# Loading each 128-token block with its own DMA, 4 KB reads on the DRAM side

## The chip, the cores and the metric

One core of a Trainium2 chip. The metric is the time of one execution in microseconds on the device; lower is better.

## The reference, cut to what matters

```python
def _attn_ref(x, f_logit, lower_bound):        # x, f_logit: (4, 6336, 256) float32
    f = lower_bound + (1.0 - lower_bound) * sigmoid(f_logit)
    i = 1.0 - f
    for t in range(S):                         # a recurrence along the sequence
        h = f[:, t] * h + i[:, t] * x[:, t]
        y[:, t] = h
def _moe_ref(x, w_h, w_t, b_t):                # on y, 25344 tokens x 256
    H = maximum(x @ w_h, 0);  T = sigmoid(x @ w_t + b_t)
    return T * H + (1 - T) * x
```

52 MB are read and 26 MB written.

## The kernel before

The work is cut into 25 units. Unit 0 has 768 tokens; units 1 to 24 have 1,024 tokens each, as eight blocks of 128. The loads of a full unit are two DMAs of 1 MB on the sync queue (SP); its output goes out in two stores of 512 KB on the same queue. Names: `lt` is f_logit in SBUF, `xt` is x, `u` the sigmoid (the gate), `bv` the product u*x, `y` the scan, `d` and `e` two multiplications after it, `o` the output. In the profile's lines PE is TensorE, PEld its weight loads, DVE VectorE, ACT ScalarE, POOL GpSimd; a q behind a name (SPq) is the list of instructions that issues for that engine.

```python
inp  = tc.tile_pool(name="inp",  bufs=4)      # lt, xt, u: four buffers each
outp = tc.tile_pool(name="outp", bufs=2)      # o: two buffers

def load(n):
    ...
    for src, t in ((f_logit, lt), (x, xt)):
        if len(segs) == 1:                    # a full unit
            b, s0, _, ln = segs[0]
            pin(nc.sync.dma_start(t, src[b, s0:s0 + ln, :].rearrange("(j p) d -> p j d", p=np_)))
        else: ...                             # unit 0: two loads of 384 KB per tensor

def gate(n):    ... ScalarE: u = sigmoid(-lt)           # reads all of lt
def product(n): ... GpSimd: bv = u * xt, in four pieces
def scan(n, h): ... VectorE: y = scan(f, bT)            # 1,024 steps, two halves h
def o_act(n, q):
    ... ScalarE: o[:, half q] = copy(PSUM)
    nc.sync.dma_start(out_bsd[b, a:a + ln // 2, :].rearrange("(j p) d -> p j d", p=np_), oq)

for n in range(-3, NU + 2):                   # one iteration, cut:
    load(n + 4)
    ... o_act(n - 2, 0) ... gate(n + 2) ... o_act(n - 2, 1) ...
    ... product(n + 2)                        # each engine runs its part in this order
```

All DMAs of this program (they are issued by SyncE and ScalarE) share eight completion semaphores in turn (numbers 100 to 107 in the trace), and a ninth DMA is not issued until the oldest of the eight has landed: in the traces before the change no DMA is issued with more than seven others out. At the start this is a wait of 3.0 us (below).

Of the kernel before, what the change touches and what calls it, by code (L numbers as in the profile page):

```python
# [19 lines left out]
def kernel(  # L20
# [16 lines left out]
    nc = tc.nc  # L37
    B, S, D = x.shape
# [3 lines left out]
    NB = 8  # L42
# [21 lines left out]
    def pin(ins):  # L64
        return tc.keep_in_program_order(ins)

    def load(n):
        np_, segs = units[n]
        lt = inp.tile([P, NB, D], FP32, tag="lt")
        xt = inp.tile([P, NB, D], FP32, tag="xt")  # L70
        for src, t in ((f_logit, lt), (x, xt)):
            if len(segs) == 1:
                b, s0, _, ln = segs[0]
                pin(nc.sync.dma_start(t, src[b, s0:s0 + ln, :].rearrange("(j p) d -> p j d", p=np_)))
            else:
                t4 = t.rearrange("p (b j) d -> p b j d", j=2)
                for j in range(2):
                    nc.sync.dma_start(
                        t4[:np_, :, j, :],
                        src[:, j * np_:(j + 1) * np_, :].rearrange("b p d -> p b d"))  # L80
        st[n]["lt"], st[n]["xt"] = lt, xt

    load(0)
    load(1)

    ident_b = singles.tile([P, P], BF16, name="ident_b")
# [7 lines left out]
    for h in range(NH):  # L94
        for vec, t in ((lower_bound, lb), (moe_b_t, bt)):
            nc.scalar.dma_start(t[:, h:h + 1], bass.AP(
                tensor=vec.tensor, offset=vec.offset + h * P, ap=[[1, P], [1, 1]]))
# [149 lines left out]
    for n in range(-3, NU + 2):  # L247
        if ok(n + 4) and n + 4 > 1:
            load(n + 4)
# [70 lines left out]
```

## Time and profile before

| | before |
|---|---|
| time, median of 2 (range) | 236.41 us (235.45 to 237.36) |
| one unit in steady state | 8.19 us (spacing of the e products) |
| VectorE busy there | 39.5 of 40 us |
| DMA rate there | 384 GB/s; the highest of the page's 40 slices is 388 |

The busy time of each engine in three stretches of steady state (busy us and number of instructions per engine, then the granted clock, the DMA share and GB/s):

```profile
core 0: us, PE busy (x) PEld busy (x) DVE busy (x) ACT busy (x) POOL busy (x), PEclk, DMA share, GB/s
60.00:100.00 40.00, 36.59 (x398) 25.79 (x397) 39.48 (x25) 38.41 (x35) 21.70 (x20) 1.00 1.09 384
100.00:140.00 40.00, 36.96 (x395) 25.81 (x393) 39.48 (x25) 38.39 (x35) 21.70 (x20) 1.00 1.09 384
```

VectorE (DVE) is full, ScalarE (ACT) nearly so, and the DMA engines are full too. The chain of waits, by engine and line:

```profile
DVE 77%; issue 6%; PE 5%; ACT 2%; DVEq 0%; ACTq 0%
DVE y L161 45%; DVE d L199 20%; DVE e L206 12%; PE zp L175 1%; PE gp L190 1%; ACT o L233 1%; ACT t L183 1%; PE op L224 1%; PE op L223 1%; PE bT L150 0%; PE uT L136 0%; DVE e L209 0%; DVEq L206 0%; ACTq L233 0%; DVEq L209 0%
```

VectorE's scan and its two multiplications carry the chain ("issue" is time in which the engine waited for nothing that the profile shows); no DMA is on it. The DMA issues (count, size, median us from issue to landing):

```profile
DMA packets 78805, 78.68 MB, mean 334 GB/s; under 512 B 2240, under 2 KB 78784, under 8 KB 78784
...
lt<-in_f_logit_dram SPq DMA_DIRECT2D x24, 1024.0 KB, 9.3
xt<-in_x_dram SPq DMA_DIRECT2D x24, 1024.0 KB, 10.6
out_dram<-o SPq DMA_DIRECT2D x48, 512.0 KB, 7.9
```

The sync queue in one unit of steady state (start, duration, what):

```profile
64.76 1.28 SPq L74 DMA_DIRECT2D lt<-in_f_logit_dram  x1
66.13 2.57 SPq L74 DMA_DIRECT2D xt<-in_x_dram  x1
68.79 4.23 SPq L237 DMA_DIRECT2D out_dram<-o  x2
```

An issue of 1 MB takes 2.57 us, which is 1 MB at 408 GB/s: the queue is not working that long, it is held back while the DMA engines still have work: 105 to 160 rows of 1 KB are queued for each of them (5th to 95th percentile at an issue from 60 to 180 us, counted in the packet records). It is ahead of them. And two waits of the sync queue:

```profile
SPq L237 <- ACT o L233: 58.6, 28, 4.5
...
SPq L78 <- DMA lb<-in_lower_bound_dram: 3.0, 1, 3.0
```

The second is the limit of eight: the third load of the queue waits 3.0 us for the tiny lower_bound load, which has nothing to do with it, at a time when eight DMAs are out. In the trace's semaphore numbers the two share one (100).

### The profile page before, as it was taken

To read this page: it belongs to the slowest core of one execution; us is meant where nothing else is said; L and a number is where in the kernel's file an instruction comes from. 1 tells how busy PE (TensorE), PEld (TensorE's weight loads), DVE (VectorE), ACT (ScalarE), POOL (GpSimd) and SP (SyncE) were. 2 spreads that over 40 slices of the span, in tenths; PEclk is the share of its full clock that TensorE was granted. 3 is DMA by queue.
4 is the path that set the end of the run, shared out by engine and by line. 5 is a ranking of instruction groups with operands and counts; after the bars stand their busy time and mean duration, and the time that the engine had idled before them with its cause. 6 is when DMAs were issued, how large, how long until landed. Compare 5 with 4: busy or idle time off the path is not lost.

```text
span 235.8 us, 4853 instructions
## 1 busy us (share of the span) xinstructions
PE 192.1 (81%) x2000; PEld 134.5 (57%) x2000; DVE 203.6 (86%) x144; ACT 198.3 (84%) x176; POOL 114.2 (48%) x108
## 2 busy tenths in 40 slices
PE   0135899898999989899998989898999989897751
PEld 0125566666566666667566666656666666665441
DVE  0425799999999999999999999999999999999540
ACT  0645789999999999999999999999999999975541
POOL 1088553574376357436634753673475357430000
PEclk9999999999999999999999999999999999999985
DMA  6999999999999999999999999999999995243255
GB/s 150 302 386 386 386 383 386 379 385 383 382 386 383 386 382 386 384 384 379 386 386 382 385 383 383 379 382 375 385 383 386 388 368 205 97 152 119 89 178 177
DMA packets 78805, 78.68 MB, mean 334 GB/s; under 512 B 2240, under 2 KB 78784, under 8 KB 78784
## 3 DMA queue, kind: packets, MB, share of 16 engines
q1 hardware_dynamic: 77664, 77.86, 94.4%
q10 hardware_dynamic: 1120, 0.53, 0.9%
q8 instruction: 15, 0.25, 0.4%
q14 instruction: 6, 0.05, 0.0%
HBM read 52.43 MB, written 25.95 MB: 332 GB/s over the span
## 4 chain that ended last, share of the span: by engine, by line
DVE 77%; issue 6%; PE 5%; ACT 2%; DVEq 0%; ACTq 0%
DVE y L161 45%; DVE d L199 20%; DVE e L206 12%; PE zp L175 1%; PE gp L190 1%; ACT o L233 1%; ACT t L183 1%; PE op L224 1%; PE op L223 1%; PE bT L150 0%; PE uT L136 0%; DVE e L209 0%; DVEq L206 0%; ACTq L233 0%; DVEq L209 0%
## 5 line engine op out<-in xcount | busy, mean ns | idle before, releaser
L126 POOL TENSOR_TENSOR bv<-u,xt 128x512 bf16<-128x512 f16 (+1 forms) x100 | 113.2, 1164 | 93.7 <-DVE e L206 72.9
L161 DVE TENSOR_TENSOR_SCAN y<-f,y,bT 128x1024 bf16<-128x1024 f16 x48 | 112.3, 2341 | 2.6 <-ACT t L183 1.4
L183 ACT ACTIVATE t<-zp,bt 128x1024 bf16<-128x1024 f32 (+1 forms) x50 | 55.3, 1106 | 13.6 <-PE zp L175 10.6
L199 DVE SCALAR_TENSOR_TENSOR d<-y,ncc,gp 128x1024 bf16<-128x1024 bf16 (+1 forms) x50 | 62.2, 1244 | 2.5 <-PE gp L190 2.5
L144 ACT ACTIVATE f<-uT,ncc 128x1024 f16<-128x1024 f16 (+1 forms) x50 | 55.9, 1117 | 5.5 <-PE uT L136 5.5
L233 ACT COPY o<-op 128x1024 f32<-128x1024 f32 (+1 forms) x50 | 50.2, 1005 | 5.7 <-PE op L224 5.7
L190 PE MATMUL gp<-y,w_sb 128*128 128x512 bf16 (+1 forms) x200 | 51.5, 380 | 4.0 <-DVE d L199 1.4
L223 PE MATMUL op<-diag,y 128*128 128x128 f16 (+1 forms) x400 | 50.9, 221 | 2.2 <-ACT o L233 2.2
L175 PE MATMUL zp<-y,w_sb 128*128 128x512 bf16 (+1 forms) x200 | 51.6, 381 | 0.3 <-ACT t L183 0.3
L224 PE MATMUL op<-ident_b,e 128*128 128x128 bf16 (+1 forms) x400 | 50.8, 221 | 0.5 <-DVE e L206 0.5
L119 ACT ACTIVATE u<-lt 128x2048 f16<-128x2048 f32 (+1 forms) x25 | 47.5, 1902 | 2.1 <-DMA lt<-in_f_logit_dram 2.1
L150 PE MATMUL bT<-ident_b,bv 128*128 128x128 bf16 (+1 forms) x400 | 31.7, 222 | 20.8 <-DVE y L161 16.5
L224 PEld LDWEIGHTS <-e 128*128 128x128 bf16 (+1 forms) x400 | 39.7, 100 | 8.8 <-DVE e L206 1.9
L223 PEld LDWEIGHTS <-y 128*128 128x128 bf16 (+1 forms) x400 | 39.8, 100 | 5.7
L150 PEld LDWEIGHTS <-bv 128*128 128x128 bf16 (+1 forms) x400 | 26.8, 99 | 27.5 <-issue 20.0
L136 PE MATMUL uT<-ident_h,u 128*128 128x128 f16 (+1 forms) x400 | 32.2, 227 | 11.0 <-ACT u L119 10.0
L190 PEld LDWEIGHTS <-w_sb 128*128 128x128 f16 x200 | 19.6, 98 | 24.4 <-issue 7.1
L136 PEld LDWEIGHTS <-u 128*128 128x128 f16 (+1 forms) x400 | 26.0, 103 | 11.4 <-ACT u L119 10.0
L206 DVE TENSOR_TENSOR e<-d,t 128x2048 bf16<-128x2048 bf16 x24 | 29.4, 1225 | 2.9 <-DVE d L199 0.5
L175 PEld LDWEIGHTS <-w_sb 128*128 128x128 f16 x200 | 18.7, 99 | 18.2 <-issue 1.1
L161 DVE TENSOR_TENSOR_SCAN y<-f,bT 128x192 bf16<-128x192 f16 x8 | 3.8, 534 | 7.3 <-PE bT L150 7.3
L119 ACT ACT_TABLE_LOAD x1 | 1.3, 1283 | 6.7 <-DMA lt<-in_f_logit_dram 6.7
(15 smaller groups left out, 5.7 us busy)
## 6 DMA issues: line engine op xcount, KB each, us to landing
lt<-in_f_logit_dram SPq DMA_DIRECT2D x24, 1024.0 KB, 9.3
xt<-in_x_dram SPq DMA_DIRECT2D x24, 1024.0 KB, 10.6
out_dram<-o SPq DMA_DIRECT2D x48, 512.0 KB, 7.9
lt<-in_f_logit_dram SPq DMA_DIRECT2D x2, 384.0 KB, 5.0
xt<-in_x_dram SPq DMA_DIRECT2D x2, 384.0 KB, 5.7
out_dram<-o SPq DMA_DIRECT2D x2, 384.0 KB, 6.6
w_raw<-in_moe_w_h_dram ACTq DMA_DIRECT2D x1, 256.0 KB, 4.8
w_raw<-in_moe_w_t_dram ACTq DMA_DIRECT2D x1, 256.0 KB, 5.4
```

The lines of the kernel that those rows point to most:

```text
L126: ins = pin(nc.gpsimd.tensor_mul(bv[:np_, q:q + 2], st[n]["u"][:np_, q:q + 2], st[n]["xt"][:np_, q:q + 2]))
L136: pin(nc.tensor.transpose(uT[:, j * np_:(j + 1) * np_], st[n]["u"][:np_, j, h * P:(h + 1) * P], ident_h[:np_, :np_]))
L144: pin(nc.scalar.activation(st[n]["f"][:, h, :N], st[n]["uT"][:, :N], AF.Identity, scale=ncc[:, h:h + 1], bias=1.0))
L150: pin(nc.tensor.transpose(bT[:, j * np_:(j + 1) * np_], st[n]["bv"][:np_, j, h * P:(h + 1) * P], ident_b[:np_, :np_]))
L161: pin(nc.vector.tensor_tensor_scan(y[:, h, c0:c0 + ln], st[n]["f"][:, h, c0:c0 + ln], st[n]["bT"][:, c0:c0 + ln], 0.0 if prev is None else ...
L175: pin(nc.tensor.matmul(zp[:, i, :e - a], w_sb[:, 1, ki, m * P:(m + 1) * P], y[:, ki, a:e], start=ki == 0, stop=ki == NH - 1))
L183: pin(nc.scalar.activation(st[n]["t"][:, m, :, :w], st[n]["zp"][:, :, :w], AF.Sigmoid, bias=bt[:, m:m + 1]))
L190: pin(nc.tensor.matmul(gp[:, i, :e - a], w_sb[:, 0, ki, m * P:(m + 1) * P], y[:, ki, a:e], start=ki == 0, stop=ki == NH - 1))
L199: pin(nc.vector.scalar_tensor_tensor(st[n]["d"][:, m, :, :w], y2, ncc[:, m:m + 1], st[n]["gp"][:, :, :w], op0=ALU.mult, op1=ALU.max))
L206: ins = pin(nc.vector.tensor_mul(e, st[n]["d"], st[n]["t"]))
L223: pin(nc.tensor.matmul(o, y[:, h, j * np_:(j + 1) * np_], diag[:, h], start=True, stop=False))
L224: pin(nc.tensor.matmul(o, e[:, h, i, c:c + np_], ident_b, start=False, stop=True))
```

## The change

Its intent: each block of 128 tokens is 128 KB in one run of DRAM, so it can be read in 4 KB pieces (four tokens of 1 KB) while SBUF still gets 1 KB per partition. For that each block needs its own DMA.

```diff
-                pin(nc.sync.dma_start(t, src[b, s0:s0 + ln, :].rearrange("(j p) d -> p j d", p=np_)))
+                for j in range(NB):
+                    a = s0 + j * np_
+
+                    pin(nc.sync.dma_start(t[:, j], bass.AP(
+                        tensor=src.tensor, offset=src.offset + (b * S + a) * D, ap=[[4 * D, np_ // 4], [1, 4 * D]])))
```

A full unit now has 16 loads of 128 KB and 2 stores of 512 KB on the sync queue: 18 issues instead of 4.

## The prediction

> What bounds it now. Between 40 and 200 us the kernel repeats every 8.19 us, one unit of 1,024 tokens (spacing of the e products in the chain of waits). VectorE fills it: from 60 to 180 us it is busy 39.5 of every 40 us and shows no wait over 0.15 us; two scans of 2.34, two d of 1.25, one e of 1.23 us (they overlap a little). The chain is 77% VectorE. ScalarE is at 38.4 of 40 us. The DMA engines are as full: 3.15 MB a unit in 8.19 us is 384 GB/s and the slices never exceed 386. But the DMA is not late: in steady state each f_logit block lands 10.5 to 11.7 us before its sigmoid starts; no steady wait names a load.
>
> What the change does.
> Removed: the 1 KB reads on the DRAM side of 48 MB. A 1 KB packet costs 42.4 ns of an engine (16 x 1,024 B / 386 GB/s). [...] VectorE alone needs 8.19 us, so this saving is off the critical path.
> Added: 384 issues instead of 48, so 18 instead of 4 per unit on the sync queue. An issue that isn't held back by full queues took 0.31 to 0.39 us (0.37 for late stores), plus about 0.04 us between two: 18 x 0.36 to 0.42 = 6.5 to 7.6 us of 8.19. Nearly full, but it fits.
> Moved: in-flight depth. At the start the sync queue's third load waits 3.0 us for the landing of the unrelated lower_bound load, when eight DMAs are out; a ninth waits for the oldest. Before, 4 or 5 of up to 1 MB are out; now eight of mostly 128 KB. A lone 512 KB store lands 2.8 us after its issue, 1.36 us of it transfer, so about 1.4 us is latency. A hand count with these numbers gives a free-running cycle of the sync queue of 7.8 to 8.4 us. The lead of 11 us lets it be 0.2 to 0.4 us too slow for twenty units without VectorE waiting.
>
> Head: loads of units 1 and 2 are just in time (0.0 to 0.8 us). They will arrive at the rate of the issues (about 330 GB/s, not 386), but the first product can start on the first two blocks. I expect -0.5 to +1.5 us. Tail (from 200 us): no loads, unchanged.
>
> Prediction: 236.8 us, 234.8 to 246 in 8 of 10; faster by over 2% 0.03, within 2% 0.72, slower by over 2% 0.25.
>
> Right if: the e products stay 8.19 us apart; VectorE still 39.5 of 40 us busy; no steady waits on loads; load packets over 2 KB; 18 issues a unit of 0.3 to 0.4 us; a load lands 2 to 5 us after its issue, not 9 to 11; its lead over its use smaller but positive.
>
> Wrong if: an issue with its gap takes 0.46 us or more, so that 18 exceed 8.19 us: then sigmoid and product wait for loads and the period is the sync queue's (0.50 us would be about 9 us, +5 to 8%). The same follows if depth eight starves the engines, or if 4 KB reads into four 1 KB rows move less than about 365 GB/s. More semaphore waits on ScalarE (eight DMAs per sigmoid), which has only 4% to spare, could also show. It is faster only if VectorE's own work shrinks, which nothing here does.

Its 365 GB/s is an estimate; it agrees with 3.15 MB in 8.19 + 0.4 us, the most that I let the queue be too slow.

## More of the kernel before

The runs of the kernel before lie between 235.45 and 238.02 us, about 1% apart. Each run comes with a state, fast or slow.

The sync queue is one list in program order: loads of unit n+4, then the two stores of unit n-2.

## The result, and the profile after

| | before | after |
|---|---|---|
| time, median of 2 (range) | 236.41 us (235.45 to 237.36) | 292.20 us (290.97 to 293.43) |
| ratio, 95% interval | | 1.236 (1.205 to 1.267) |
| one unit in steady state | 8.19 us | 10.8 us (mean of 60 to 240 us) |

Ratios here are the mean time of one kernel's fast runs over that of the other's of the same rounds, so they are not quite the ratios of the medians. Executions over 1.5% slower than the fastest of the same kernel are left out of the means.

The change is 24% slower. The same stretches after the change:

```profile
60.00:100.00 40.00, 27.72 (x275) 20.18 (x275) 26.45 (x17) 28.25 (x26) 13.62 (x13) 0.88 0.92 290
100.00:140.00 40.00, 30.80 (x319) 22.08 (x318) 30.75 (x19) 29.00 (x28) 18.07 (x16) 0.96 0.92 296
```

No engine is full any more, and the DMA moves 290 to 296 GB/s instead of 384. The chain:

```profile
SPq 30%; DMA 27%; ACT 24%; issue 10%; DVE 4%; PE 2%; POOL 2%; POOLq 0%; ACTq 0%; DVEq 0%
```

The sync queue's issues and the DMAs have taken VectorE's place. The DMA packets and issues:

```profile
DMA packets 84186, 78.75 MB, mean 270 GB/s; under 512 B 7616, under 2 KB 84160, under 8 KB 84160
...
lt<-in_f_logit_dram SPq DMA_DIRECT2D x192, 128.0 KB, 3.3
xt<-in_x_dram SPq DMA_DIRECT2D x192, 128.0 KB, 3.1
out_dram<-o SPq DMA_DIRECT2D x48, 512.0 KB, 4.3
```

All packets are still under 2 KB (in the records: 1,024 bytes, like before), so the 4 KB reads don't show in the packets at all. What grew is the number of packets under 512 B: 5,376 more, 16 for each of the 336 additional DMAs. The added ones are of 4 bytes. I take them for completion marks, since the trace also shows 16 semaphore updates for each DMA. The sync queue in one unit, and what its load line costs (duration in ns, minimum/median/maximum):

```profile
121.19 0.94 SPq L241 DMA_DIRECT2D out_dram<-o  x2
122.18 5.08 SPq L77 DMA_DIRECT2D lt<-in_f_logit_dram  x8
127.36 3.69 SPq L77 DMA_DIRECT2D xt<-in_x_dram  x8
131.15 0.94 SPq L241 DMA_DIRECT2D out_dram<-o  x2
```

```profile
L77 SPq DMA_DIRECT2D lt<-in_f_logit_dram x192: 327/432/1838, 6.4 to 245.5; - x192
L77 SPq DMA_DIRECT2D xt<-in_x_dram x192: 327/430/1902, 11.5 to 249.3; - x192
```

The queue issues without a break: 121.19 to 131.15 us is one unit, all of it issuing. Adding up the records of the sync queue from 60 to 240 us (302 issues, in steady state):

```
part of a unit of 18 issues                                   us
18 issues at 0.430 us, and 18 gaps of 0.044 us               8.53
issue time beyond 0.430 us ("held", most in the loads
  right after the two stores)                                2.03
waits                                                        0.13
sum                                                         10.69   (measured spacing 10.78)
```

The landings keep this pace. By the median of 15 units, the two stores of a unit land in 2.8 us and its 16 loads in 7.9 us, 265 GB/s.

In the same stretch the queue waited 2.1 us in all: it is the busiest thing in the program. Who waits because of it (total us, times, longest us):

```profile
POOL bv L130 <- ACT u L123: 114.5, 18, 13.8
...
ACT o L237 <- DMA out_dram<-o: 64.8, 19, 10.7
...
DVE e L210 <- ACT t L187: 50.5, 19, 9.9
```

ScalarE's copy into `o` waits once a unit for a store, because only two output buffers exist and the stores stand in the sync queue behind 16 loads. In steady state the first store of a unit is issued about 15 us after its copy has ended (before: 1.6 to 2.9 us). ScalarE runs its list in order, so the sigmoids behind the copy wait too (ScalarE stands still for 3.56 us before the copy at 116.05 us), then GpSimd's product (114.5 us in all, above) and VectorE (50.5). The loads are not late: f_logit lands about 10 us before its sigmoid starts, nearly as early as before.

Where the 55.8 us of the span went, by the first output copy of a unit: unit 2's starts at 62.05 us instead of 49.77 (12.3 us lost in the start; 10.7 of it is one wait for unit 0's store, which stands behind the prefetch of six units), and from there to unit 19 the kernel takes 183.4 us instead of 139.2 (44.2 us, 2.6 us a unit). The tail gives 0.6 back.

### The profile page after: what moved, and what is told of

Its sections match the earlier page's. It is cut to its first block, busy times and chain, and to the rows that moved or that the text cites. A ratio compares the mean times of both kernels' runs of the same rounds, so it can differ in the third digit from the quotient of the medians.

```text
span 291.6 us, 5339 instructions
## 1 busy us (share of the span) xinstructions
PE 199.5 (68%) x2000; PEld 139.9 (48%) x2000; DVE 205.5 (70%) x144; ACT 195.7 (67%) x176; POOL 114.2 (39%) x108
## 4 chain that ended last, share of the span: by engine, by line
SPq 30%; DMA 27%; ACT 24%; issue 10%; DVE 4%; PE 2%; POOL 2%; POOLq 0%; ACTq 0%; DVEq 0%
SPq L77 27%; DMA lt<-in_f_logit_dram 21%; ACT f L148 8%; ACT t L187 7%; ACT o L237 6%; DMA xt<-in_x_dram 5%; ACT u L123 4%; SPq L241 2%; DMA out_dram<-o 2%; POOL bv L130 2%; DVE y L165 2%; DVE d L203 1%; DVE e L210 1%; PE gp L194 1%; PE zp L179 1%
## 5 line engine op out<-in xcount | busy, mean ns | idle before, releaser
L130 POOL TENSOR_TENSOR bv<-u,xt 128x512 bf16<-128x512 f16 (+1 forms) x100 | 113.1, 1164 | 150.5 <-ACT u L123 114.5
L227 PE MATMUL op<-diag,y 128*128 128x128 f16 (+1 forms) x400 | 52.6, 225 | 64.8 <-ACT o L237 64.8
L228 PEld LDWEIGHTS <-e 128*128 128x128 bf16 (+1 forms) x400 | 40.5, 102 | 76.9 <-issue 73.3
L210 DVE TENSOR_TENSOR e<-d,t 128x2048 bf16<-128x2048 bf16 x24 | 29.4, 1225 | 51.4 <-ACT t L187 50.5
L203 DVE SCALAR_TENSOR_TENSOR d<-y,ncc,gp 128x1024 bf16<-128x1024 bf16 (+1 forms) x50 | 62.2, 1245 | 2.5 <-PE gp L194 2.5
L187 ACT ACTIVATE t<-zp,bt 128x1024 bf16<-128x1024 f32 (+1 forms) x50 | 55.9, 1117 | 5.6 <-PE zp L179 5.6
L194 PE MATMUL gp<-y,w_sb 128*128 128x512 bf16 (+1 forms) x200 | 53.9, 394 | 1.5 <-DVE d L203 1.4
L228 PE MATMUL op<-ident_b,e 128*128 128x128 bf16 (+1 forms) x400 | 52.8, 225 | 0.5 <-DVE e L210 0.5
L227 PEld LDWEIGHTS <-y 128*128 128x128 bf16 (+1 forms) x400 | 40.4, 101 | 5.7
L140 PE MATMUL uT<-ident_h,u 128*128 128x128 f16 (+1 forms) x400 | 34.2, 235 | 11.6 <-ACT u L123 9.9
L154 PE MATMUL bT<-ident_b,bv 128*128 128x128 bf16 (+1 forms) x400 | 34.4, 234 | 8.4 <-DVE y L165 4.3
L140 PEld LDWEIGHTS <-u 128*128 128x128 f16 (+1 forms) x400 | 28.5, 107 | 13.2 <-ACT u L123 9.9
L194 PEld LDWEIGHTS <-w_sb 128*128 128x128 f16 x200 | 19.7, 103 | 20.8 <-issue 4.5
L179 PEld LDWEIGHTS <-w_sb 128*128 128x128 f16 x200 | 19.5, 99 | 20.2 <-issue 2.2
```

Source lines behind the costliest of these rows:

```text
L130: ins = pin(nc.gpsimd.tensor_mul(bv[:np_, q:q + 2], st[n]["u"][:np_, q:q + 2], st[n]["xt"][:np_, q:q + 2]))
L140: pin(nc.tensor.transpose(uT[:, j * np_:(j + 1) * np_], st[n]["u"][:np_, j, h * P:(h + 1) * P], ident_h[:np_, :np_]))
L179: pin(nc.tensor.matmul(zp[:, i, :e - a], w_sb[:, 1, ki, m * P:(m + 1) * P], y[:, ki, a:e], start=ki == 0, stop=ki == NH - 1))
L187: pin(nc.scalar.activation(st[n]["t"][:, m, :, :w], st[n]["zp"][:, :, :w], AF.Sigmoid, bias=bt[:, m:m + 1]))
L194: pin(nc.tensor.matmul(gp[:, i, :e - a], w_sb[:, 0, ki, m * P:(m + 1) * P], y[:, ki, a:e], start=ki == 0, stop=ki == NH - 1))
L203: pin(nc.vector.scalar_tensor_tensor(st[n]["d"][:, m, :, :w], y2, ncc[:, m:m + 1], st[n]["gp"][:, :, :w], op0=ALU.mult, op1=ALU.max))
```

## The experiments

Theories, by their letters in the expectations. A: the issues themselves; each takes the sync queue 0.47 us. B: the uneven split (4 KB into 1 KB rows) makes the issue or the transfer slow. C: the order of the queue and the two output buffers. D, formed after the sixth run (e6_fourteen): small loads are issued too slowly to keep the DMA engines busy, and the engines have no spare time to win it back.

All runs beside runs of the kernel before on the same chip:

```
run                issues/unit  time us   ratio to before (95%)     us/unit  verdict
after                   18      292.20    1.236 (1.205 to 1.267)     10.8    slower
e1_rows                 18      292.78    1.233 (1.224 to 1.242)     10.7    slower
e2_four                 10      236.35    0.998 (0.992 to 1.004)      8.19   same
e3_gpstore           16+2*      278.75    1.177 (1.169 to 1.185)     10.1    slower
e4_outbufs              18      285.57    1.204 (1.195 to 1.213)     10.9    slower
e5_smallstore (wrong)   18      264.71    1.120 (1.115 to 1.126)      9.19   slower
e6_fourteen             14      274.22    1.159 (1.154 to 1.165)      9.95   slower
e9_eleven               11      276.40    1.167 (1.160 to 1.173)     10.2    slower
e10_eleven_small (wrong)11      237.82    1.006 (1.000 to 1.011)      8.19   same
e11_sixteen_small (wrong)16+2*  247.14    1.039 (1.036 to 1.043)      8.60   slower
e7_const                 4      236.03    1.000 (0.996 to 1.003)      8.19   same
e8_const_four           10      241.61    1.023 (1.020 to 1.027)      8.19   unclear
                   * the two stores on GpSimd's queue     (wrong): wrong result on purpose
```

A verdict says faster or slower from 2% on. The interval of e8_const_four begins just under that (1.0196), so its verdict is unclear, though it is slower beyond the noise.

### e1_rows: the same eight loads with 1 KB rows on both sides

```diff
-                    pin(nc.sync.dma_start(t[:, j], bass.AP(
-                        tensor=src.tensor, offset=src.offset + (b * S + a) * D, ap=[[4 * D, np_ // 4], [1, 4 * D]])))
+                    pin(nc.sync.dma_start(t[:, j:j + 1], src[b, a:a + np_, :].rearrange("(j p) d -> p j d", p=np_)))
```

> The same eight loads of 128 KB per block, but both sides of each are 128 rows of 1 KB (no 4 KB reads). Theory A, the number of issues: an issue costs the sync queue 0.47 us with its gap whatever the rows are, 18 of them and some 2 us of held-back issues make a unit of 10.7 us: time within 2% of 292 us. Theory B, the uneven split of 4 KB reads into 1 KB rows makes the issue or the transfer slow: the issue falls to about 0.33 us plus 0.04 us, 18 fit into 8.19 us, time 236 to 240 us. In between (0.40 us of pitch, period near 8.3 to 9 us, 240 to 255 us) would mean both.

Measured: 292.78 us, the same as the change. Back-to-back issues take 0.430 us here too, and the 16 loads of a unit land in 7.87 us against 7.91 with 4 KB reads (medians). B is out: the shape of the reads neither costs nor gains anything that shows. The whole effect is the cutting into eight.

### e2_four: four loads of 256 KB per tile

```diff
-                for j in range(NB):
+                for j in range(0, NB, 2):
                     a = s0 + j * np_
-                    ...                   # the changed kernel's load of one block
+                    pin(nc.sync.dma_start(t[:, j:j + 2], src[b, a:a + 2 * np_, :].rearrange("(j p) d -> p j d", p=np_)))
```

> Four loads of 256 KB per tile with 1 KB rows on both sides, so 10 issues a unit instead of 18. Theory A: 10 x 0.47 = 4.7 us, even with 2 us held back below 8.19 us, so 236 to 238 us and VectorE full again. Theory B says the same for this one. If it is still above 245 us, something other than the issue's own time (the depth of eight, or the splitting itself) costs.

Measured: 236.35 us, the same as before. Stretches of this run:

```profile
60.00:100.00 40.00, 36.60 (x397) 25.87 (x396) 39.48 (x26) 38.51 (x35) 21.69 (x20) 1.00 1.09 382
100.00:140.00 40.00, 36.60 (x396) 25.72 (x394) 39.48 (x25) 38.37 (x36) 21.69 (x21) 1.00 1.09 383
```

VectorE is full again and the DMA moves 382 GB/s; the eight loads of a unit land in 5.5 us instead of 7.9. Twice the bytes per issue turn a 24% loss into none.

### e3_gpstore: the stores on GpSimd's queue

```diff
-            nc.sync.dma_start(out_bsd[b, a:a + ln // 2, :]....
+            nc.gpsimd.dma_start(out_bsd[b, a:a + ln // 2, :]....
```

> The changed loads as they are, but the stores of the full units are issued by GpSimd, so the sync queue has 16 loads a unit and nothing else. Theory A: 16 x 0.474 = 7.6 us fits into 8.19 us if the held-back issues go with the stores: 236 to 243 us. Theory B in its transfer form (the engines move only 290 GB/s with the uneven split): 3.15 MB a unit still need 10.8 us, so 285 us or more. Theory C, stores wait behind 16 loads and only two output buffers exist: 236 to 243 us too, since they wait no more.

Measured: 278.75 us, a miss for A as I had put it and for C. The 16 loads still lose time: in the sync queue's records from 60 to 230 us the held time is 2.0 us a unit, as before the move, though no store is on that queue any more. So the holding does not come from standing behind a store in the queue. Issues, held time and waits (0.5 us) again add up to the 10.1 us of a unit. The run is not clean: the semaphore records show that the stores on GpSimd's queue use eight semaphores of their own (111 to 118), so the limit of eight is eased too, and GpSimd's product now stands behind its stores, which wait for ScalarE's copies (92.6 us in 26 waits).

### e4_outbufs: four output buffers instead of two

```diff
-    outp = ctx.enter_context(tc.tile_pool(name="outp", bufs=2))
+    outp = ctx.enter_context(tc.tile_pool(name="outp", bufs=4))
```

> The changed kernel with four output buffers instead of two, so ScalarE's copy need not wait for the store of two units before. Theory A: the sync queue stays full all the time, so the period stays 10.7 us and the time within 2% of 292 us; the wait only moves elsewhere (to the loads). Theory C, the buffers and the order make the loop: 260 us or less.

Measured: 285.57 us, 2.3% less than the change, a bit more than the 2% that I had allowed. The start no longer stops (unit 2's first copy starts at 51.5 us instead of 62.1), but the period stays at 10.9 us; the wait has moved to the loads, whose lead of 10 us is now 0.1 to 0.3 us. The wait for the stores was only where the full queue was felt. C explains part of the start and nothing of the period.

### e5_smallstore: stores of a quarter of the bytes (wrong result)

```diff
-            nc.sync.dma_start(out_bsd[b, a:a + ln // 2, :].rearrange("(j p) d -> p j d", p=np_), oq)
+            nc.sync.dma_start(out_bsd[b, a:a + np_, :], oq[:, 0])
```

> The changed kernel with the same 18 issues a unit, but each store of a full unit writes only its first 128 tokens (128 KB instead of 512 KB); the result is wrong on purpose. Theory A1, the back-to-back pitch of 0.474 us alone keeps the queue full and the held-back issues (2.0 us a unit) come from the stores' bytes: the held-back time vanishes, the period is 18 x 0.474 = 8.5 us, time 242 to 250 us. Theory A2, the issues are held back by the loads themselves or by their count: period still above 10 us, time 280 us or more.

Measured: 264.71 us, between the two expectations. The period is 9.19 us: 8.53 us of bare issues, about 0.75 held (it was 2.03), nearly no waits; this sums to 9.3. So the bare issues alone already exceed VectorE's 8.19 us, and most of the held time goes with the stores' bytes. My time was too low because I had left out the held rest and the start, where unit 2's copy again waits until 62.2 us.

### e6_fourteen: f_logit in eight loads, x in four

```diff
+                g = 1 if t is lt else 2
+                for j in range(0, NB, g):
+                    ... t[:, j:j + g] <- src[b, a:a + g * np_, :]
```

> f_logit in eight loads and x in four per tile, 14 issues a unit, all bytes moved. If issue time adds up as in the changed kernel (0.474 us each plus 2.0 us held back a unit): 14 x 0.474 + 2.0 = 8.6 us, so 242 to 250 us. If the held-back time fell with the queue less busy, it is below 8.19 us and the time is 236 to 238 us. If depth of eight or the DMA itself set the pace, it stays above 260 us.

Measured: 274.22 us. The first two expectations fail and the third holds: over 260 us, which it puts down to the depth of eight or the DMA itself. 14 issues are only 6.7 us of bare issue time, yet the unit takes 9.95 us. Held time is 2.2 us, and now 1.2 us a unit are waits for a landing: the limit of eight. Bare issues and the 2.0 us held before do not explain this run, which led to theory D. It is an argument from numbers: an issue of 128 KB every 0.474 us feeds 276 GB/s to engines that need 384 all the time. Such a phase leaves them idle, and at 388 GB/s at most they hardly catch up.

### e9_eleven and e10_eleven_small: the test of theory D

```diff
+                g = 1 if t is lt else NB          # f_logit in eight loads, x in one
...
-            nc.sync.dma_start(out_bsd[b, a:a + ln // 2, :].rearrange("(j p) d -> p j d", p=np_), oq)
+            nc.sync.dma_start(out_bsd[b, a:a + np_, :], oq[:, 0])     # e10 only
```

> f_logit in eight loads of 128 KB, x in one of 1 MB: 11 issues a unit. Theory A, the sum of issue times (11 x 0.474 = 5.2 us plus 2.0 us held back = 7.2 us): below 8.19 us, 236 to 238 us. Theory D, the DMA engines starve while small loads are issued (128 KB per 0.474 us is 276 GB/s against 386) and have no spare time to win it back: 1 MB in small loads takes 3.8 us instead of 2.7, the unit 2.7 + 3.8 + 2.7 = 9.2 us at least, so 255 to 265 us although the sync queue has few issues.

> As e9_eleven, with stores of a quarter of the bytes (wrong on purpose), which gives the DMA engines 2 us of spare time in a unit. Theory D: 3.8 + 2.7 + 0.7 = 7.2 us is below 8.19 us, so VectorE sets the pace again: 236 to 239 us. If e9_eleven is slow for another reason (depth of eight, held issues), this one stays above 245 us.

Measured: e9 takes 276.40 us with one issue more than e2, and e10, with the same 11 issues and less to store, 237.82 us. The stretches of e9 and then of e10:

```profile
100.00:140.00 40.00, 31.71 (x302) 21.34 (x300) 30.54 (x20) 28.89 (x27) 15.96 (x15) 0.85 0.94 297
```

```profile
100.00:140.00 40.00, 37.06 (x386) 25.43 (x386) 39.48 (x26) 37.91 (x35) 21.62 (x20) 1.00 0.95 293
```

In e10 the DMA moves 293 GB/s, as slow as in the changed kernel, but that is all that it has to move, and VectorE is full. In e9 it has to move 384 and moves 297 to 317, by stretch. So the number of issues is not the cause by itself. But e9's loss was more than D's 255 to 265 us, and the landings of e9 contradict D's account of where the time goes. By the median of 14 units from 60 to 200 us, the eight small loads land in 2.7 us (D: 3.8), the two stores in 2.8 us, and the one big x load 4.6 us after the small load before it (D: 2.7). The small loads, queued behind the stores, move at the full rate (1 MB in 2.7 us, 388 GB/s); the big one does not (1 MB in 4.6 us, 228 GB/s). The sync queue of e9 shows what closes its loop:

```profile
SPq L77 <- DMA out_dram<-o: 36.2, 34, 2.5
SPq L77 <- DMA xt<-in_x_dram: 21.4, 21, 1.9
```

```profile
135.87 1.08 SPq L240 DMA_DIRECT2D out_dram<-o  x2
137.00 8.50 SPq L77 DMA_DIRECT2D lt<-in_f_logit_dram  x8
145.61 0.38 SPq L77 DMA_DIRECT2D xt<-in_x_dram  x1
```

Eight f_logit loads take 8.50 us to issue, mostly waiting. The big x load and the two stores hold three of the eight semaphores until they land, five small loads take the rest, and the sixth waits for x, the seventh and eighth for the stores. In the semaphore records these three issues follow the three landings within 0.03 us in 12 of 14 units. The next x stands behind the eighth small load, and so behind the landing of the second store. From one x to the next it takes x's time from issue to landing (6.9 us), the two stores (2.8 us) and one more small issue (about 0.4 us): 10.1 us, against a period of 10.2. So in e9 the limit of eight sets the pace. What is not shown is why x lands so late. In half-microsecond bins of the packet records the engines move 223, 204 and 129 GB/s from 137.0 to 138.5 us, although x and both stores had been issued by 136.94 us.

The pair therefore leaves D unproven. Small stores shorten this loop as well: in e10 x takes 6.2 us from issue to landing and the stores 0.7, so the loop is about 7.4 us and VectorE's 8.19 us decide. The expectation that depth of eight would keep e10 above 245 us had overlooked this. In the changed kernel, where no x load is big, the queue hardly waits for a landing (0.13 us a unit) and the loads land at the pace of their issues, as D says; there D and A describe the same full queue.

### e11_sixteen_small: small stores on GpSimd's queue (wrong result)

The edits of e3 and e5 together.

> The changed loads, with stores of a quarter of the bytes issued by GpSimd (wrong on purpose): the sync queue has 16 issues a unit and the DMA engines 2 us of spare time. If the back-to-back pitch of 0.474 us is the floor of the small-store run with 18 issues (period 9.19 us), 16 x 0.474 = 7.6 us plus about 0.6 us held is at or just under 8.19 us: 236 to 242 us. If something else set those 9.19 us (compute waiting on more semaphores, say), it stays at 260 us or more.

Measured: 247.14 us, period 8.60 us (median 8.19). Two issues fewer on the sync queue take the period from 9.19 to 8.60 us, so the bare issue time was the floor of e5 (the stores' own eight semaphores can't have done it: e5's queue waited less than 0.1 us a unit); the estimate of 236 to 242 us was too low, since 0.8 us a unit are still held and 0.25 are waits.

### e7_const and e8_const_four: is the wait at the start worth anything?

```diff
-    for h in range(NH):
-        for vec, t in ((lower_bound, lb), (moe_b_t, bt)):
-            nc.scalar.dma_start(t[:, h:h + 1], ...)
+    for vec, t in ((lower_bound, lb), (moe_b_t, bt)):
+        nc.scalar.dma_start(t, bass.AP(tensor=vec.tensor, offset=vec.offset, ap=[[1, P], [P, NH], [1, 1]]))
```

e7 is the kernel before with this edit, e8 is e2_four with it.

> The kernel before, with lower_bound and the bias loaded by one DMA each instead of two, so that only eight DMAs come before the first big loads and the third load of the sync queue need not wait for a landing. If the eight in flight are a limit of the program: the x loads of unit 0 start 2 to 3 us earlier, the first product about 1.5 us earlier, and the whole is 0.5 to 2 us faster than before (ratio 0.992 to 0.998). If the wait at the start had another cause or the bandwidth of the start decides, no change.

> As e7_const, and the loads in four pieces per tile as in e2_four (10 issues a unit). If the finer arrival helps the start at all, it is faster than e7_const by up to 1 us; if not, the same as e7_const within 0.5%.

Measured: in e7 unit 0's x loads are issued at 1.7 and 2.2 us instead of 4.7 and 5.3, so the wait of the third load was indeed the limit of eight. But they land only 0.5 us earlier (10.8 instead of 11.3 us), the start gains 0.55 us, and the time is the same (ratio 1.000). So the wait itself was worth little; that the engines' rate at the start decides instead is my reading, and not tested. e8 is 2.3% slower, a miss, and its VectorE tells where. First e8's, then e2's weight preparation:

```profile
14.85 5.78 DVE L114 SCALAR_TENSOR_TENSOR w_sb<-w_raw,cc,ndiag 128x128 f16<-128x128 f32 x1
```

```profile
9.42 0.34 DVE L115 SCALAR_TENSOR_TENSOR w_sb<-w_raw,cc,ndiag 128x128 f16<-128x128 f32 x1
```

The weights land 2.6 us later in e8 (which I put down to the x loads, issued earlier), so this preparation falls beside GpSimd's products (11.46 to 20.48 us in e8) and one instruction takes 5.78 us instead of 0.34; the first scan starts at 21.1 instead of 16.4 us. The three instructions just before it, from 11.54 us, slow down too (1.15 to 1.23 us instead of 0.24 to 0.28), and the last two, from 20.55 us, after the products, take 0.27 and 0.35 us again. In e2 all of them end before the products begin at 11.34 us. That the products beside it slow this preparation is my reading of these times; no run tests it alone. It does not hold for every VectorE instruction: in steady state of the kernel before, d takes 1.25 us beside a product (at 107.60 us) and away from one (102.84).

No version beats the kernel before: e2_four and e7_const are equal to it within the noise.

## Why the prediction was wrong, point by point

- Right: VectorE sets the pace before, and landing to use stays positive (10 us) with landings mostly 2 to 5 us after the issue (median 3.3). None of it decided the time. That the 4 KB reads changed nothing was right by luck: the prediction wanted load packets over 2 KB, and they stayed at 1,024 bytes, so there was no saving to lie off the critical path, and no run here tests what larger packets would have saved. Its "the slices never exceed 386" was a misreading: one slice of the page, 183 to 189 us, is 388.
- Wrong term 1, "18 x 0.36 to 0.42 = 6.5 to 7.6 us". It is 18 x 0.474 = 8.53 us, above VectorE's 8.19. I took the time of an issue from issues that stood alone: 0.31 us after a 3 us wait, 0.37 for a late store. In the changed kernel 13 loads that follow a gap of over 0.2 us take 0.33 us as well (median), but the 352 that follow at once take 0.43 (median). In this kernel the full queue runs at the second number. The trace of before had it in sight: the six DMAs in a row on ScalarE's queue took 0.41 to 0.50 us each.
- Missing term 2: the issues held back while the stores' megabyte drains, 2.03 us a unit. My hand count knew only a full queue or a wait for a landing. e5 shows that it shrinks to about 0.75 us with the stores' bytes, e3 that it doesn't depend on the stores' queue. It is the larger term: of the 2.6 us that a unit lost, the bare issues account for 0.3 (8.53 instead of 8.19), the held ones for 2.0. Why they are held stays open.
- Wrong step 3, "The lead of 11 us lets it be 0.2 to 0.4 us too slow for twenty units". The lead protects loads. The stores share the queue behind 16 loads and have two buffers; ScalarE stopped for them while the loads still led by 10 us. With four buffers (e4) the lead was used up and the period did not change. No lead pays for 2.6 us a unit over 17 units.
- Wrong step 4, the start: I expected -0.5 to +1.5 us and it lost 12.3, of which 10.7 is one wait for unit 0's store behind the prefetch.
- What I did name as a danger was the cause: "An issue with its gap takes 0.46 us or more". Its price was too small (5 to 8%), as I counted no held issues. More semaphore waits on ScalarE (the other danger) don't show: its wait is for the stores.
- The step behind the wrong terms: I asked whether 18 issues fit into 8.19 us, as if queue and DMA engines overlapped freely. The DMA had 384 of at most 388 GB/s in use. Bytes per issue over issue time, 128 KB / 0.474 us = 276 GB/s, was a number to compare with it: the loads then landed at 265 GB/s. 256 KB per issue passes that test and ran as before (e2). The mixed sizes (e6, e9) were slow as well, but there the limit of eight took part, so they don't prove this test.

Left open: what exactly holds an issue after the stores (fewer rows are queued then, 30 to 77 per DMA engine, than the 105 to 160 of the kernel before); why the big x load of e9 and e10 moves slowly; and why the granted clock is 0.85 in e9's profiled run although TensorE is less busy (its other runs had 0.96 to 0.98 and took as long, so the clock is not what made e9 slow). No run issued the small loads from two queues, which would have tested the full queue most directly.

## What to carry to other kernels

Before cutting a DMA into pieces, divide the bytes of one piece by the back-to-back time of an issue (0.474 us here) and compare with the rate that the kernel needs: here loads of 128 KB throughout (276 GB/s) failed where 384 are needed, and loads of 256 KB throughout passed. It is a first check and no proof: e6 and e9 were slow with larger loads among the small. Take the issue time from issues in a row, not from ones that stand alone, and multiply the piece by the number of DMAs that may be in flight (eight here, so 1 MB in pieces of 128 KB) to see how far the queue can run ahead. This queue, in program order, carried its lateness to the stores, which stand last in it: they were issued about 15 us after their copies, while the loads led by 10 us.
